# Sparse attention with a dense layer behind it: q and k turned by transposing DMAs instead of by fp32 products

## The chip, the cores and the metric

The kernel runs on one core of a Trainium2 chip. A core has five engines that run side by side, each through its own instructions in order: PE (matrix products, with weight loads shown as PEld), VectorE (DVE in the profile), ScalarE (ACT), GpSimd (POOL) and SyncE (SP), which here only issues DMAs. Data lies in SBUF (128 partitions) and products come out in PSUM banks. The metric is the device time of one execution in microseconds, lower is better. The median of the runs is compared.

## The reference, cut to what matters

Sixty-four heads (batch 8 x 8 heads) of 576 tokens with 64 features go through attention with a threshold: per query only those scores count that lie within tau = 0.02 of the row's largest. The result, in fp32, goes through a dense layer with a leaky ReLU.

```python
scores = scale * np.matmul(q, k.transpose(0, 1, 3, 2))        # 576 x 576 per head
thresh = np.max(scores, axis=-1, keepdims=True) - tau
scores = np.where(scores >= thresh, scores, -1000000000.0)
scores = scores - np.max(scores, axis=-1, keepdims=True)
attn = np.exp(scores)
attn = attn / (np.sum(attn, axis=-1, keepdims=True) + 1e-09)
attn_out = np.matmul(attn, v)
x = attn_out.transpose(0, 2, 1, 3).reshape(B * S, H * D)      # 4608 x 512
h = x @ w_in                                                  # 512 -> 2048
out = np.maximum(0.01 * h, h) @ w_out                         # 2048 -> 512
```

The threshold makes the scores delicate: they have to be near fp32. The kernel gets this from fp16 products by splitting q and k into two fp16 halves, hi and lo (hi = fp16(64 x), lo = fp16(64 x - hi)), and adding hi*hi + lo*hi + hi*lo.

## The kernel before, in words

**Rounds and steps.** Two heads make a pair (32 pairs), since two times 64 features fill 128 partitions. The main loop (L406 on) runs over rounds c of two pairs, and each round over nine steps t. A step takes 128 queries of the two heads of a pair: t = 0 to 3 the first pair's, t = 4 to 7 the second's, t = 8 the last 64 of each. There are 16 rounds with scores and one more that drains what is left. The program is written in the order in which each engine runs it (manual_schedule); no planner moves anything.

**A step.** `s_mm` (L145) multiplies the halves on PE into two PSUM tiles `s`, one per head. There are only two such tiles, so the next step's products wait until this step's have been read. `s_max` (L167) reads one head's tile on VectorE, writes the scaled negative scores `sn` and their row minimum `nmx` (L181), and lets GpSimd add tau: `nth`, one column (L186). ScalarE then takes the exponential, `e` (L191); for some second heads it also does the masking by itself (L197, L201: "direct" in the code). One step later `s_mask` (L206) masks on VectorE (L214: `sn` and `e` from SBUF, `W` out, one instruction for each head that ScalarE hasn't masked, so one or two per step) and SP issues a transposing DMA of `W` into `wT` (L220). In the next round, at t = 3 and 5, `values` (L271) multiplies `wT` by v, and VectorE scales the result into `xT` (L289), of which GpSimd copies 64 columns.

**The dense layer** is cut into units (`h_unit` L296, `out_mm` L310) that fill PE between the score products; `work` (L375) gives each step its number of them by a table of shares.

**q and k.** `load_qk` (L73) loads a pair's q and k in fp32 with tokens on the partitions into one of three `nat` buffers: nine chunks of 128 tokens, four of q, four of k, and one with the last 64 of both. The loads are issued by SP about a round ahead. But the products need features on the partitions. `prep` (L122) turns a pair in two parts, four chunks (i = 0, 512 columns) and five (i = 1, 640 columns): a PE product with the fp32 identity `I32` per chunk (L129) into the PSUM pair "A", then ScalarE writes `hi` from it (L138), and VectorE writes `lo` (L139), put off by the list `soon` to the end of the step. In round c the pairs of the next round are turned at t = 6 (first pair, part 0), 7 (first pair, part 1), 8 (second pair, part 0), and at t = 0 of the following round (second pair, part 1). The PSUM pair "A" also serves `values` and the row sums (`sums_3`, `sums_4`).

The queues in a step: VectorE does `sn`, `sn`, the masks of the step before, then what `soon` holds (`xT`, `lo`). GpSimd does `nth`, `nth`, then small copies and, in even rounds from t = 4 on, the issue of v loads. SP issues the transposes of W, the q and k loads and the output stores, in order.

Of the kernel before, what the change touches and what calls it, by code (L numbers as in the profile page):

```python
# [10 lines left out]
FP16 = mybir.dt.float16  # L11
OP = mybir.AluOpType
AF = mybir.ActivationFunctionType
# [3 lines left out]
def kernel(  # L17
# [10 lines left out]
    nc = tc.nc  # L28
# [3 lines left out]
    NP = B * H // 2  # L32
    NG = H // 2
    NC = NP // 2
    NT = 9
    NJ = d_ff // 128
    QS = 64.0
    BS = 1.0 / (QS * QS * 8.0)
    RS = 1.0 / 2048.0
# [2 lines left out]
    sb = ctx.enter_context(tc.tile_pool(name="sb", bufs=1))  # L42
# [18 lines left out]
    nat, qk, wTs, xTs = {}, {}, {}, {}  # L61
# [49 lines left out]
    soon = []  # L111

    def take(fs):
        r = list(fs)
        fs.clear()
        return r

    def run(fs):
        for f in fs:
            f()  # L120

    def prep(p, i, tag="A", bufs=1):  # L122


        t = nat[p]
        pt = pair_of_banks(tag, bufs).rearrange("p a b -> p (a b)")
        for c in range(4 + i):

            nc.tensor.matmul(  # L129
                out=pt[0:128, ds(c * 128, 128)],  # L130
                lhsT=t[0:128, 4 * i + c, :, :].rearrange("p h d -> p (h d)"),
                rhs=I32[:, :],
                is_transpose=True, skip_group_check=True,
            )
        N = 512 + 128 * i
        hi = sb.tile([128, N], FP16, tag=f"hi{i}", bufs=3, name=f"hi{i}")
        lo = sb.tile([128, N], FP16, tag=f"lo{i}", bufs=3, name=f"lo{i}")
        nc.scalar.activation(out=hi[:, :], in_=pt[:, 0:N], func=AF.Copy, bias=0.0, scale=QS)  # L138
        soon.append(lambda: nc.vector.scalar_tensor_tensor(  # L139
            out=lo[:, :], in0=pt[:, 0:N], scalar=QS, in1=hi[:, :],  # L140
            op0=OP.mult, op1=OP.subtract,
        ))
        qk.setdefault(p, {})[i] = (hi, lo)

    def s_mm(c, t):  # L145


        out = [ps.tile([128, 2, 512], FP32, tag="s", bufs=2, name="s") for _ in range(2)]
        if t < 8:
            srcs = [(2 * c + t // 4, 0, ds(t % 4 * 128, 128), ds(0, 128))]  # L150
        else:
            srcs = [(2 * c + e, 1, ds(576, 64), ds(64 * e, 64)) for e in range(2)]
        for half in range(2):
            for ti, (a, b) in enumerate(((0, 0), (1, 0), (0, 1))):
                for p, i, cols, po in srcs:
                    for h in range(2):
                        r = ds(h * 64, 64)
                        nc.tensor.matmul(  # L158
                            out=out[h][po, half, 0:288], lhsT=qk[p][i][a][r, cols],
                            rhs=qk[p][1][b][r, ds(half * 288, 288)],  # L160
                            start=(ti == 0), stop=(ti == 2), skip_group_check=True,
                        )
        sc[(c, t)] = out
# [146 lines left out]
    def out_mm(key, g_in, part, osb, half, store):  # L310
# [64 lines left out]
    def work(n):  # L375
        for _ in range(min(n, len(units))):
            units.pop(0)[1]()

    with tc.manual_schedule():
        nc.scalar.preload_act_table_set("natural_log_exp_and_others")  # L380
        for i, tail in ((0, 0), (1, 0), (0, 1), (1, 1)):
# [6 lines left out]
            out=sel[:, :, :], in0=I32[:, 0:18].unsqueeze(2).to_broadcast([128, 18, 64]),  # L388
            in1=I32[:, 64:82].unsqueeze(2).to_broadcast([128, 18, 64]), op=OP.add,
# [16 lines left out]
        for c in range(NC + 1):  # L406
            last = c == NC
            for t in range(NT):
                step = c * NT + t
                if c > 1 and c % 2 == 0 and t == 6:  # L410

                    if c % 4 == 2 and c > 2:
                        push_tail(c // 2 - 3, 1)
                    push_main(c // 2 - 1)
                    if c % 4 == 0:
                        push_tail(c // 2 - 2, 0)
                    if last:
                        push_tail(c // 2 - 2, 1)
                if not last:
                    s_mm(c, t)  # L420


                nxt = {6: (2 * c + 2, 0), 7: (2 * c + 2, 1), 8: (2 * c + 3, 0), 0: (2 * c + 1, 1)}
                if c == 0:
                    nxt[0], nxt[1] = (1, 0), (1, 1)
                pi = nxt.get(t)
                if pi is not None and pi[0] >= NP:
                    pi = None
                if c == 0 and t < 2:
                    prep(*pi)  # L430
                    pi = None

                if c > 0 and t in (3, 5):
                    values(c - 1, t // 2 - 1)

                ahead = [share[i % NT] for i in range(step, (c // 2 * 2 + (0 if c % 2 == 0 and t < 6 else 2)) * NT + 6)]
                credit = min(credit, 1.0) + (len(units) - credit) * share[t] / sum(ahead)
                n = min(int(credit + 0.01), len(units))
                credit -= n
                if not last:  # L440


                    direct = tau_f <= 16.0 and (
                        t not in (3, 7) if c < 3 else t in (3, 5) or not any(u[0] for u in units[:n]))
                    s_max(c, t, 0, False)
                if c > 0 and t == 1:
                    sums_1(c - 1)
                work(n - n // 2)
                if pi is not None:
                    prep(*pi)  # L450
                if c > 0 and t in (2, 4):
                    sums_4(c - 1, t // 2 - 1)
                if not last:
# [63 lines left out]
```

## Time and profile before

| what | value |
|---|---|
| median of 3 runs | 540.81 us (540.47 to 541.48) |
| span of the profiled execution | 538.3 us, 12333 instructions |
| PE busy | 497.8 us (92%) |
| VectorE busy | 421.7 us (78%) |
| ScalarE busy | 433.8 us (81%) |
| GpSimd busy | 188.1 us (35%) |
| DMA of SP's queue, share of 16 engines | 72.3% |
| fp32 products that turn q and k (L129) | 288 in all, 9 a pair |
| transposing DMAs (L220) | 144, issue 1.354 us (median), 3.9 us to landing (median) |

The runs time the whole execution; the profile's span is that of one profiled execution, from its first to its last instruction, and lies 2.5 us under the median. An engine's share is an average over the whole span. The granted clock of PE is 0.80 in the first 60 us and 1.00 from about 100 us on, and after about 487 us only the dense layer is left.

In the groups, a row names the line, the engine and the operation, the tile written and the tiles read, shapes and count; then busy time in us and the mean of one in ns; then the idle time of the engine before these instructions and what ended it.

### The profile page before, as it was taken

To read this page: it belongs to the slowest core of one execution; us is meant where nothing else is said; L and a number is where in the kernel's file an instruction comes from. 1 tells how busy PE (TensorE), PEld (TensorE's weight loads), DVE (VectorE), ACT (ScalarE), POOL (GpSimd) and SP (SyncE) were. 2 spreads that over 40 slices of the span, in tenths; PEclk is the share of its full clock that TensorE was granted. 3 is DMA by queue.
4 is the path that set the end of the run, shared out by engine and by line. 5 is a ranking of instruction groups with operands and counts; after the bars stand their busy time and mean duration, and the time that the engine had idled before them with its cause. 6 is when DMAs were issued, how large, how long until landed. Compare 5 with 4: busy or idle time off the path is not lost.

```text
span 538.3 us, 12333 instructions
## 1 busy us (share of the span) xinstructions
PE 497.8 (92%) x4384; PEld 272.8 (51%) x4384; DVE 421.7 (78%) x1106; ACT 433.8 (81%) x765; POOL 188.1 (35%) x430
## 2 busy tenths in 40 slices
PE   5678679899999999999999999999999999999996
PEld 3345454454545565454545566455545566445444
DVE  4897989988899878987899878987899878982000
ACT  3887879899878989889888989889888989884622
POOL 0754556443433334222432234323432234331000
PEclk9676969999999999999999999999999999999999
DMA  6999999998998699778999799777998699654001
GB/s 151 150 202 161 175 182 214 200 180 173 172 165 136 139 169 196 140 137 153 183 155 143 132 182 185 142 135 159 183 155 136 132 187 135 111 89 106 39 40 58
DMA packets 266814, 80.50 MB, mean 150 GB/s; under 512 B 251905, under 2 KB 264193, under 8 KB 266753
## 3 DMA queue, kind: packets, MB, share of 16 engines
q1 hardware_dynamic: 249136, 70.68, 72.3%
q0 software_dynamic: 17536, 8.92, 14.2%
q8 instruction: 34, 0.56, 0.4%
q14 instruction: 28, 0.22, 0.1%
q10 hardware_dynamic: 80, 0.13, 0.1%
HBM read 36.70 MB, written 9.44 MB: 86 GB/s over the span
## 4 chain that ended last, share of the span: by engine, by line
PE 43%; ACT 25%; DVE 16%; issue 8%; DMA 4%; POOL 3%; SPq 0%; DVEq 0%; ACTq 0%; POOLq 0%
PE u L316 13%; DVE sn L181 11%; PE u L301 10%; PE s L158 10%; PE A L279 8%; ACT e L191 7%; ACT far L197 5%; ACT W L201 5%; DVE W L214 3%; ACT gM L305 3%; ACT hi L138 3%; POOL nth L186 3%; DMA nat<-in_q_dram 2%; DVE lo L139 1%; ACT rc L268 1%
## 5 line engine op out<-in xcount | busy, mean ns | idle before, releaser
L181 DVE TENSOR_SCALAR_CACHE_REDUCE sn<-s 128x576 f32<-128x576 f32 x288 | 206.5, 750 | 49.3 <-PE s L158 49.1
L186 POOL TENSOR_SCALAR nth<-nmx 128x1 f32<-128x1 f32 x288 | 127.4, 442 | 251.7 <-DVE sn L181 229.5
L191 ACT ACTIVATE e<-sn,nmx 128x576 f16<-128x576 f32 x196 | 150.5, 769 | 32.4 <-DVE sn L181 32.2
L214 DVE SCALAR_TENSOR_TENSOR W<-sn,nth,e 128x576 f16<-128x576 f32 x196 | 155.6, 814 | 0.0
L301 PE MATMUL u<-xT,win 128*128 128x512 f16 x512 | 128.9, 380 | 2.5 <-ACT gM L305 2.5
L316 PE MATMUL u<-wout,gM 128*128 128x512 f16 x512 | 126.2, 380 | 0.0
L158 PEld LDWEIGHTS <-hi 64*128 64x128 f16 (+1 forms) x1280 | 65.1, 99 | 70.2 <-issue 54.9
L158 PE MATMUL s<-hi,hi 64*128 64x288 f16 x512 | 86.2, 300 | 10.3 <-DVE sn L181 8.8
L158 PE MATMUL s<-lo,hi 64*128 64x288 f16 (+1 forms) x640 | 92.2, 294 | 0.0
L158 PE MATMUL s<-hi,lo 64*128 64x288 f16 (+1 forms) x640 | 92.1, 294 | 0.0
L301 PEld LDWEIGHTS <-win 128*128 128x128 f16 x768 | 58.7, 98 | 56.5 <-issue 20.1
L305 ACT ACTIVATE gM<-u 128x512 f16<-128x512 f32 x128 | 74.6, 588 | 11.7 <-PE u L301 11.7
L197 ACT ACTIVATE far<-sn,nth 128x576 f32<-128x576 f32 x92 | 71.0, 771 | 13.8 <-POOL nth L186 11.6
L201 ACT ACTIVATE W<-far,ntau 128x576 f16<-128x576 f32 x92 | 71.3, 775 | 3.0
L316 PEld LDWEIGHTS <-gM 128*128 128x128 f16 x512 | 44.7, 98 | 51.3 <-issue 12.3
L139 DVE SCALAR_TENSOR_TENSOR lo<-A,hi 128x512 f16<-128x512 f32 (+1 forms) x63 | 47.6, 756 | 14.2 <-ACT hi L138 13.7
L129 PE MATMUL A<-I,nat 128*128 128x128 f32 x283 | 44.6, 288 | 9.9 <-DVE lo L139 4.7
L279 PE MATMUL A<-wT,V 128*64 128x288 f16 x640 | 47.5, 297 | 1.5 <-ACT rc L268 1.1
L129 PEld LDWEIGHTS A<-I,nat 128*128 128x128 f32 x283 | 35.2, 147 | 25.2 <-DVE lo L139 10.0
L138 ACT ACTIVATE hi<-A 128x512 f16<-128x512 f32 (+1 forms) x63 | 40.0, 636 | 7.6 <-PE A L129 7.6
L279 PEld LDWEIGHTS <-V 128*64 128x64 f16 x640 | 36.6, 113 | 11.9 <-issue 8.4
L158 PEld LDWEIGHTS <-lo 64*128 64x128 f16 (+1 forms) x640 | 32.1, 99 | 12.6 <-issue 8.9
(44 smaller groups left out, 292.1 us busy)
## 6 DMA issues: line engine op xcount, KB each, us to landing
nat<-in_q_dram SPq DMA_DIRECT2D x32, 256.0 KB, 3.8
nat<-in_k_dram SPq DMA_DIRECT2D x32, 256.0 KB, 3.9
out_dram<-osb SPq DMA_DIRECT2D x16, 512.0 KB, 3.0
wT<-W SPq DMA_TRANSPOSE x144, 3.9
V<-in_v_dram POOLq DMA_DIRECT2D x8, 256.0 KB, 6.1
win<-in_moe_w_in_dram POOLq DMA_DIRECT2D x16, 128.0 KB, 5.2
V<-in_v_dram POOLq DMA_DIRECT2D x16, 128.0 KB, 4.7
wout<-in_moe_w_out_dram POOLq DMA_DIRECT2D x16, 128.0 KB, 4.3
```

Of the source, the lines that this page charges most:

```text
L129: nc.tensor.matmul(out=pt[0:128, ds(c * 128, 128)], lhsT=t[0:128, 4 * i + c, :, :].rearrange("p h d -> p (h d)"), rhs=I32[:, :], is_transp ...
L158: nc.tensor.matmul(out=out[h][po, half, 0:288], lhsT=qk[p][i][a][r, cols], rhs=qk[p][1][b][r, ds(half * 288, 288)], start=(ti == 0), stop= ...
L181: nc.vector.tensor_scalar(out=sn[:, h, :].rearrange("p (a b) -> p a b", a=2), in0=s_[:, :, 0:288], scalar1=-BS, scalar2=None, op0=OP.mult, ...
L186: nc.gpsimd.tensor_scalar(out=nth[:, h:h + 1], in0=nmx[:, h:h + 1], scalar1=1.0, scalar2=tau_f, op0=OP.mult, op1=OP.add,)
L191: nc.scalar.activation(out=e[:, h, :], in_=sn[:, h, :], func=AF.Exp, bias=nmx[:, h:h + 1], scale=-1.0,)
L197: nc.scalar.activation(out=far[:, :], in_=sn[:, h, :], func=AF.Prelu, bias=nth[:, h:h + 1], scale=-1.0, alpha=BIG,)
L201: nc.scalar.activation(out=w[:, ds(h * 576, 576)], in_=far[:, :], func=AF.Exp, bias=ntau[:, 0:1], scale=1.0, accum_out=dens[c][:, 2 * t + ...
L214: nc.vector.scalar_tensor_tensor(out=w[:, ds(h * 576, 576)], in0=sn[:, h, :], scalar=nth[:, h:h + 1], in1=e[:, h, :], op0=OP.is_le, op1=OP ...
L279: nc.tensor.matmul(out=t[ds(h * 64, 64), half, 0:288], lhsT=vb[:, g, h, kb, :], rhs=wT[:, 4 * h + kb, ds(e * 576 + half * 288, 288)], star ...
L301: nc.tensor.matmul(out=t[:, ts(j, N)], lhsT=w_in16[:, gi, ts(j0 + j, 128)], rhs=xs[gi], start=(gi == 0), stop=(gi == NG - 1), skip_group_c ...
L305: nc.scalar.activation(out=g_out, in_=t[:, 0:nj * N].rearrange("p (j n) -> p j n", j=nj), func=AF.Prelu, bias=0.0, scale=1.0, alpha=0.01)
L316: nc.tensor.matmul(out=t[:, :], lhsT=g_in(j), rhs=w_out16[:, j, :], start=(j == 0), stop=(j == NJ - 1), skip_group_check=True,)
```

## The change

The first four pairs stay as they were (`PEP = 4`). From the fifth on a pair is split where it lies, with tokens on the partitions: `split` writes `hn` = fp16(64 x) on GpSimd from `nat`, and by `soon` VectorE writes `ln` from `nat` and `hn`, in two parts of 512 and 640 columns. `turn` then has SP issue two transposing DMAs, `hn` into `hi` and `ln` into `lo`, each of 128 x 1152. In round c the next round's first pair is split at t = 4 and 5 and turned at the end of t = 5; the second is split at t = 7 and 8 and turned at the end of t = 0 of the next round. `hn` and `ln` have one buffer each. `hi` and `lo` are now one tile per pair of nine chunks, in three buffers, where there were two tiles of four and five chunks; the score products read the same columns. Of the 288 fp32 products 36 are left, of the 64 ScalarE copies 8; VectorE has as many instructions as before, GpSimd has 56 more, SP issues 56 DMAs more.

```diff
+    PEP = 4
...
+    halves = {}
+
+    def turned(p):
+        if p not in qk:
+            qk[p] = [sb.tile([128, 9, 128], FP16, tag=n, bufs=3, name=n) for n in ("hi", "lo")]
+        return qk[p]
...
-        hi = sb.tile([128, N], FP16, tag=f"hi{i}", bufs=3, name=f"hi{i}")
-        lo = sb.tile([128, N], FP16, tag=f"lo{i}", bufs=3, name=f"lo{i}")
-        nc.scalar.activation(out=hi[:, :], in_=pt[:, 0:N], func=AF.Copy, bias=0.0, scale=QS)
+        hi, lo = (x.rearrange("p c q -> p (c q)")[:, ds(512 * i, N)] for x in turned(p))
+        nc.scalar.activation(out=hi, in_=pt[:, 0:N], func=AF.Copy, bias=0.0, scale=QS)
...
+    def split(p, i):
+
+        if i == 0:
+            halves[p] = [sb.tile([128, 1152], FP16, tag=n, bufs=1, name=n) for n in ("hn", "ln")]
+        hn, ln = halves[p]
+        cols = ds(512 * i, 512 + 128 * i)
+        t = nat[p].rearrange("p c h d -> p (c h d)")
+        nc.gpsimd.tensor_scalar(out=hn[:, cols], in0=t[:, cols], scalar1=QS, scalar2=1.0,
+                                op0=OP.mult, op1=OP.mult)
+        soon.append(lambda: nc.vector.scalar_tensor_tensor(
+            out=ln[:, cols], in0=t[:, cols], scalar=QS, in1=hn[:, cols],
+            op0=OP.mult, op1=OP.subtract,
+        ))
+
+    def turn(p):
+
+        for x, n in zip(turned(p), halves.pop(p)):
+            nc.sync.dma_start_transpose(out=x[:, :, :], in_=n[:, :])
...
-                            out=out[h][po, half, 0:288], lhsT=qk[p][i][a][r, cols],
-                            rhs=qk[p][1][b][r, ds(half * 288, 288)],
+                            out=out[h][po, half, 0:288], lhsT=x[a][r, cols],
+                            rhs=x[b][r, ds(512 + half * 288, 288)],
...
-                if pi is not None and pi[0] >= NP:
+                if pi is not None and pi[0] >= PEP:
                     pi = None
+                si = {4: (2 * c + 2, 0), 5: (2 * c + 2, 1), 7: (2 * c + 3, 0), 8: (2 * c + 3, 1)}.get(t)
+                if si is not None and not PEP <= si[0] < NP:
+                    si = None
+                ti = {5: 2 * c + 2, 0: 2 * c + 1}.get(t)
+                if ti is not None and not PEP <= ti < NP:
+                    ti = None
...
+                if si is not None:
+                    split(*si)
                 if prev is not None:
                     s_mask(*prev)
                     prev = None
                 if not last:
                     prev = (c, t)
                 run(take(soon))
+                if ti is not None:
+                    turn(ti)
```

More of the change, by code (lines that the diff above doesn't have):

```diff
@@ L135, in prep @@
         N = 512 + 128 * i
-        hi = sb.tile([128, N], FP16, tag=f"hi{i}", bufs=3, name=f"hi{i}")
-        lo = sb.tile([128, N], FP16, tag=f"lo{i}", bufs=3, name=f"lo{i}")
-        nc.scalar.activation(out=hi[:, :], in_=pt[:, 0:N], func=AF.Copy, bias=0.0, scale=QS)
+        hi, lo = (x.rearrange("p c q -> p (c q)")[:, ds(512 * i, N)] for x in turned(p))
+        nc.scalar.activation(out=hi, in_=pt[:, 0:N], func=AF.Copy, bias=0.0, scale=QS)
         soon.append(lambda: nc.vector.scalar_tensor_tensor(
-            out=lo[:, :], in0=pt[:, 0:N], scalar=QS, in1=hi[:, :],
+            out=lo, in0=pt[:, 0:N], scalar=QS, in1=hi,
             op0=OP.mult, op1=OP.subtract,
         ))
-        qk.setdefault(p, {})[i] = (hi, lo)
+    def split(p, i):
[13 more added lines that the diff above has]
+            nc.sync.dma_start_transpose(out=x[:, :, :], in_=n[:, :])
     def s_mm(c, t):
@@ L149, in s_mm @@
         if t < 8:
-            srcs = [(2 * c + t // 4, 0, ds(t % 4 * 128, 128), ds(0, 128))]
+            srcs = [(2 * c + t // 4, ds(t % 4 * 128, 128), ds(0, 128))]
         else:
-            srcs = [(2 * c + e, 1, ds(576, 64), ds(64 * e, 64)) for e in range(2)]
+            srcs = [(2 * c + e, ds(1088, 64), ds(64 * e, 64)) for e in range(2)]
         for half in range(2):
             for ti, (a, b) in enumerate(((0, 0), (1, 0), (0, 1))):
-                for p, i, cols, po in srcs:
+                for p, cols, po in srcs:
+                    x = [y.rearrange("p c q -> p (c q)") for y in qk[p]]
                     for h in range(2):
```

## The prediction

> **What bounds the kernel now.** I read the busy shares first, then the costliest groups, then the waits, and last one whole round of the attention loop, step by step. The shares: PE works almost all the time, and VectorE and ScalarE are not far behind it.
>
> ```profile
> PE 497.8 (92%) x4384; PEld 272.8 (51%) x4384; DVE 421.7 (78%) x1106; ACT 433.8 (81%) x765; POOL 188.1 (35%) x430
> ```
>
> The groups that the change touches are the fp32 products that turn q and k, their ScalarE and VectorE halves, and GpSimd's one-column `nth`:
>
> ```profile
> L186 POOL TENSOR_SCALAR nth<-nmx 128x1 f32<-128x1 f32 x288 | 127.4, 442 | 251.7 <-DVE sn L181 229.5
> ...
> L139 DVE SCALAR_TENSOR_TENSOR lo<-A,hi 128x512 f16<-128x512 f32 (+1 forms) x63 | 47.6, 756 | 14.2 <-ACT hi L138 13.7
> L129 PE MATMUL A<-I,nat 128*128 128x128 f32 x283 | 44.6, 288 | 9.9 <-DVE lo L139 4.7
> ...
> L138 ACT ACTIVATE hi<-A 128x512 f16<-128x512 f32 (+1 forms) x63 | 40.0, 636 | 7.6 <-PE A L129 7.6
> ```
>
> Now stretches that run from one step's first `sn` to the next step's: t = 4 to 8 of round 6, then t = 0 to 3 of round 7 (start:end, length, then busy time and instructions of PE, weight load, VectorE, ScalarE, GpSimd; clock, DMA share, GB/s).
>
> ```profile
> 196.38:199.37 2.99, 2.96 (x50) 2.55 (x50) 2.18 (x6) 2.96 (x7) 1.59 (x3) 1.00 1.49 243
> 199.37:203.62 4.25, 4.18 (x65) 3.51 (x65) 3.59 (x9) 3.53 (x7) 1.56 (x5) 1.00 0.89 133
> 203.62:206.73 3.11, 3.11 (x25) 1.67 (x25) 2.79 (x7) 2.88 (x7) 1.82 (x4) 1.00 1.37 248
> 206.73:209.98 3.25, 3.25 (x38) 1.90 (x38) 3.01 (x7) 3.18 (x6) 1.52 (x3) 1.00 1.52 132
> 209.98:213.42 3.44, 3.44 (x26) 1.76 (x26) 2.79 (x7) 3.44 (x8) 1.53 (x3) 1.00 0.99 191
> 213.42:216.99 3.57, 3.57 (x28) 1.98 (x27) 3.57 (x11) 3.29 (x7) 1.10 (x3) 1.00 1.02 195
> ...
> sum 31.04, PE 30.36 PEld 18.10 DVE 27.48 ACT 27.45 POOL 12.10; mean PE 3.37 PEld 2.01 DVE 3.05 ACT 3.05 POOL 1.34
> ```
>
> PE fills 30.36 of a round's 31.04 us; but VectorE fills 27.48, so it has 3.6 us a round to lose before it is the bound. And it runs strictly in order. VectorE and GpSimd within t = 7, the fourth stretch:
>
> ```profile
> 207.42 0.75 DVE L181 TENSOR_SCALAR_CACHE_REDUCE sn<-s 128x576 f32<-128x576 f32 x1
> 208.09 0.08 DVE L181 DVE_READ_ACCUMULATOR sn<-s 128x1 f32 x1
> 208.09 0.81 DVE L214 SCALAR_TENSOR_TENSOR W<-sn,nth,e 128x576 f16<-128x576 f32 x1
> 208.84 0.08 DVE L214 DVE_READ_ACCUMULATOR W<-sn,nth,e 128x1 f32 x1
> 208.99 0.82 DVE L139 SCALAR_TENSOR_TENSOR lo<-A,hi 128x640 f16<-128x640 f32 x1
> ...
> 207.66 0.19 POOL L186 TENSOR_SCALAR nth<-nmx 128x1 f32<-128x1 f32 x1 [1.11 <-ACT W L201]
> 208.26 0.70 POOL L186 TENSOR_SCALAR nth<-nmx 128x1 f32<-128x1 f32 x1 [0.41 <-DVE sn L181]
> ```
>
> See the two `nth`: one column each, 0.19 us while VectorE does `sn`, 0.70 us while it does a mask (L214), ending at 208.96 with it. GpSimd gets nothing done beside a mask.
>
> **The change part by part.** It concerns 28 of 32 pairs: 56 splits and 56 turns, in rounds 1 to 14.
>
> *Removed from PE:* in the third stretch two runs of four L316 products start at 203.52 and, past four L129 products, at 204.83: 1.31 us, of which four products alone take 0.88 (203.52 to 204.40). So four turns cost 0.43 us, five by the same reading in t = 7 0.54. A round loses 2 x (0.43 + 0.54) = 1.94 us of PE, 14 rounds 27 us: the most that can be won.
>
> *Removed from ScalarE:* 56 `hi` copies of 0.636 us, 36 us. ScalarE's idle time is ended by `sn` and PE, so I count this at nothing; PE and VectorE cover it.
>
> *Moved on VectorE:* the halving stays, as `ln` instead of `lo`. Start to start `lo` takes 0.61 us (512 columns) and 0.74 (640); reading SBUF on both sides, like L214 (576 columns, 0.74 start to start), `ln` should cost the same. But it moves from t = 6, 7, 8, 0 to t = 4, 5, 7, 8, and now it waits for GpSimd.
>
> *Added on GpSimd:* a split of 512 or 640 columns, queued behind the step's second `nth`, hence free 2.28 us after the step's first `sn` (208.96 + 0.05 against 206.73), when the mask is over. Its price has no row. From below: 128x128 affine select 0.291 us against 0.185 for a one-column `nth` gives 0.83 ns a column (the 128x64 copy, 0.236, gives 0.8): 0.61 and 0.72 us. From above: the same operation on 18 columns (0.218) gives 1.94 ns a column: 1.18 and 1.43. I take the low ones, because 128 columns are nearest in size.
>
> The page GPSIMD Engine Reference of the Trainium skill (section Performance versus the Vector engine) says 512 elements take 769 ns in a well unrolled loop, between my ends; by it the splits would cost some 0.77 and 0.96 us and the sum below would be about 11 us higher; no row here shows a split.
>
> *The new wait:* `ln` waits for the split of its own step. Behind it on VectorE stands the next step's `sn`, for which PE's next scores wait. GpSimd's result reaches VectorE 0.07 us after its end (L235 to L240). Step lengths set by VectorE, first `sn` to next:
> - t = 4 and 7: 2.28 + 0.61 + 0.07 + 0.61 = 3.57 us; with two masks 0.74 more, 4.31.
> - t = 8: 2.28 + 0.72 + 0.07 + 0.74 = 3.81; two masks 4.55.
> - t = 5: one mask 3.81 again; two masks 4.55. The `xT` product (0.67) runs meanwhile.
> - t = 6 and 0: no halving left. One mask leaves 2.1, so the loop `sn`, `sn` (1.36), scores on PE (0.9) and their hand-overs sets some 2.4; two masks 2.84.
>
> Against the stretches: 3.57 + 4.55 + 2.4 + 3.57 + 3.81 + 2.84 = 20.74 where 20.61 stood. (These steps have 1, 2, 1, 1, 1 and 2 masks.) The same six of the next rounds: 21.04 against 20.03 (masks 1, 2, 1, 2, 1, 1), 21.48 against 20.69 (1, 1, 1, 2, 2, 2), 20.30 against 19.70 (1, 2, 1, 1, 1, 1). Mean +0.63 us; rounds repeat in this pattern, so 14 x 0.63 = +9 us. The steps t = 1 to 3 hold neither turns nor splits and keep their length. PE's gain of t = 6 and 0 is spent in t = 4, 7 and 8.
>
> *Added on SP:* 56 transposes. Issue 1.354 us each (median of `wT`), 5.4 us a round; SP now waits over 15 us a round for masks and scores, so this fits. SP is in order: turns stand right behind a step's `wT` transposes and ahead of q/k loads, which run a round ahead. Data: three transposes in the drain took some 1.8 us each at a DMA share of 0.8 to 1.0; four more add up to 7 us a round to queues already 87% shared.
>
> *The single `hn`/`ln` buffer:* the split of t = 7 may overwrite `hn` only when the turn of t = 5 has landed. From t = 5's first `sn`: mask over at 2.84, `wT` issued until 4.2, turn of `hn` lands 3.9 later (median) at 8.1, of `ln` 1.35 behind at 9.45. Wanted: 4.55 + 2.4 + 2.28 = 9.23 and, for `ln`, 9.9. It fits by 0.5 to 1 us, but landings range from 3.2 to 9.0 and there are more of them. Between 0 and 1.5 us a round I take 0.5: +7 us. Other buffers (three of `hi`/`lo`, six of W) leave four or more steps.
>
> Sum: span 538.3 + 9 + 7 = 554.3; the median of the runs, 540.81, lies 2.5 above the profiled span, so 556.8: 557 us.
>
> **The rivals.**
> 1. *VectorE's idle time takes the waits.* If the three unhidden waits (0.87 + 0.87 + 0.98 us = 2.7) fall into the 3.6 us that VectorE now idles, a round needs VectorE 30.1 and PE 28.4 of 31.04: 0.9 less, 14 rounds 13 us, 528 us. For it: 49 us of idle before `sn` until PE's scores. Against: that idle lies mostly in t = 1, 4 and 5; only two score tiles stand between the engines. It decides where the four splits of a round give back the 0.63 us above, that is where the wait for one is under some 0.71 us instead of 0.87.
> 2. *The split is slow* (1.18/1.43): 0.57 + 0.71 + 0.57 + 0.71 more a round, 36 us: 593. For it: the same operation's own slope; against: 17 columns make it.
> 3. *Turns land late.* With 1.5 to 2 us a round more at t = 7, 557 + 21 = 578. For it: stretches with DMA shares of 1.4 to 1.5; against: shares fall to 0.5 in others.
> 4. *The turns' cost is hidden and PE's gain lost elsewhere*: about 541.
>
> **How the numbers follow.** Forecast (546 to 568) 0.43, slow split 0.18, late turns 0.14, gain by rival 1 0.20, no change 0.05. A difference under 0.2% (1.1 us) can't be told from none. Slower: 0.43 + 0.18 + 0.14 = 0.75; faster 0.20; same 0.05. The range reaches from rival 1's 528 to rival 2's 593, with about 0.1 left out on each side.
>
> **What would show it.** Right: `ln` idle before, ended by `hn` on GpSimd, 0.3 to 1 us in each of t = 4, 7, 8, some 30 us in all; PE under 90% busy; PE waiting for `sn`; splits of 0.6 to 0.75 us. Waits of `hn` for a DMA would be the buffer. Wrong: splits that end while masks run, a VectorE without idle time ahead of `ln`, or rounds under 30 us.

## The result, and the profile after

The changed kernel takes 589.44 us (median of 4 runs, 588.58 to 591.52), the kernel before 540.64 us in the same comparison (539.92 to 541.48): a ratio of 1.0911, 95% interval 1.0887 to 1.0935. Ratios, here and below, leave out any run that took over 1.5% longer than the fastest of its kernel, so a ratio can lie a little under what the medians give. The forecast had the sign and not the size: +16 us were forecast, +49 us came. The range of 528 to 593 us holds the time, but its upper end was there for another reason, a slow split, which did not come.

The head of the page of after, its busy shares and the granted clock of PE in 40 slices:

```profile
span 588.1 us, 11908 instructions
...
PE 497.7 (85%) x4132; PEld 255.6 (43%) x4132; DVE 422.8 (72%) x1106; ACT 406.9 (69%) x709; POOL 237.9 (40%) x486
...
PEclk9568579799989999799989999798989999899999
```

PE has lost its 252 products and its instructions are still busy for as long as before (497.8 us then): the clock now falls again and again in the main loop, where it stood at 1.00 before, so that the same products last longer. No engine is busy over 90% of the span any more. The span of 588.1 us is 49.8 longer than before's 538.3, and PE's share of it fell from 92 to 85%.

What the engines wait for instead, from the groups of the page and from the list of waits (time in all, times, longest, in us):

```profile
L160 DVE SCALAR_TENSOR_TENSOR ln<-nat,hn 128x512 f16<-128x512 f32 (+1 forms) x56 | 42.5, 759 | 71.0 <-POOL hn L158 44.3
...
L158 POOL TENSOR_SCALAR hn<-nat 128x512 f16<-128x512 f32 (+1 forms) x56 | 46.0, 822 | 40.0 <-DMA hi<-hn 24.0
```

```profile
PE s L184 <- DVE sn L207: 65.2, 65, 5.5
DVE ln L160 <- POOL hn L158: 44.3, 41, 5.7
...
DVE ln L160 <- DMA lo<-ln: 26.7, 6, 7.1
...
POOL hn L158 <- DMA hi<-hn: 24.0, 6, 5.8
...
PEld L184 <- DMA hi<-hn: 17.7, 8, 3.6
```

Read these against each other. VectorE stands 71.0 us before `ln`, where some 30 were forecast. But 26.7 of them are six waits of up to 7.1 us for the turn of `lo`, and GpSimd's 24.0 are six waits for the turn of `hi`: the buffers `hn` and `ln` were still being read. By the trace GpSimd's six lie in t = 7 of rounds 1, 2, 6, 10, 12 and 14, VectorE's in t = 7 of rounds 2, 6, 7, 10, 11 and 12. In rounds 4 and 8 the split of t = 7 begins 0.13 us after the turn has landed as well, though the trace names no releaser there. So it is mostly the even rounds. Two odd-round stretches first (t = 6 and 7 of round 5), then t = 5, 6, 7, 8 of round 6 and t = 0 of round 7; columns as in the stretches of before (length; PE, weight load, VectorE, ScalarE, GpSimd; clock, DMA share, GB/s):

```profile
196.91:199.23 2.32, 1.92 (x17) 0.91 (x15) 2.18 (x7) 0.84 (x2) 1.07 (x3) 1.00 1.09 206
199.23:202.80 3.57, 3.57 (x38) 1.72 (x38) 2.80 (x8) 3.51 (x7) 1.50 (x3) 1.00 0.94 182
...
222.31:226.58 4.27, 4.27 (x64) 3.25 (x60) 4.27 (x12) 3.66 (x8) 2.80 (x5) 1.00 1.31 197
226.58:228.90 2.32, 2.27 (x19) 1.01 (x17) 2.18 (x8) 1.17 (x3) 1.71 (x5) 1.00 1.30 243
228.90:235.99 7.09, 4.75 (x41) 2.09 (x41) 2.79 (x8) 4.35 (x8) 2.69 (x5) 0.97 1.23 183
235.99:239.78 3.79, 2.69 (x14) 1.19 (x14) 2.91 (x8) 2.41 (x4) 2.19 (x4) 0.50 0.93 131
239.78:243.43 3.65, 3.65 (x20) 1.37 (x19) 2.92 (x9) 2.52 (x4) 1.10 (x3) 0.64 1.27 259
```

t = 7 took 3.57 us in round 5, to the hundredth what was forecast, and 7.09 in round 6, with no more work on VectorE (2.80 and 2.79 us). Behind the long step the granted clock is 0.50. The timeline of SP, GpSimd and VectorE tells what happened in between (start, duration; in brackets the idle time before):

```profile
197.00 1.31 SPq L168 DMA_TRANSPOSE hi<-hn  x1
198.40 1.39 SPq L168 DMA_TRANSPOSE lo<-ln  x1
...
201.54 0.62 POOL L158 TENSOR_SCALAR hn<-nat 128x512 f16<-128x512 f32 x1
```

```profile
226.03 2.98 SPq L246 DMA_TRANSPOSE wT<-W  x1
229.11 1.33 SPq L168 DMA_TRANSPOSE hi<-hn  x1
230.53 2.68 SPq L168 DMA_TRANSPOSE lo<-ln  x1
...
230.42 0.70 POOL L212 TENSOR_SCALAR nth<-nmx 128x1 f32<-128x1 f32 x1 [0.41 <-DVE sn L207]
234.48 0.62 POOL L158 TENSOR_SCALAR hn<-nat 128x512 f16<-128x512 f32 x1 [3.36 <-DMA hi<-hn]
...
230.25 0.81 DVE L240 SCALAR_TENSOR_TENSOR W<-sn,nth,e 128x576 f16<-128x576 f32 x1
...
235.38 0.69 DVE L160 SCALAR_TENSOR_TENSOR ln<-nat,hn 128x512 f16<-128x512 f32 x1 [4.30 <-DMA lo<-ln]
235.99 0.75 DVE L207 TENSOR_SCALAR_CACHE_REDUCE sn<-s 128x576 f32<-128x576 f32 x1
```

In round 5 SP issues the turn of `hn` 4.35 us after t = 5's first `sn` (192.65), and GpSimd's split follows its second `nth` without a wait. In round 6 the same turn goes out 6.80 us after it (222.31), since SP had been issuing one transfer after the other, and the transposes of W ahead of it took up to 2.98 us to issue instead of 1.3; GpSimd then stands 3.36 us until it has landed, VectorE 4.30 us, and the next `sn` behind both.

Where the 49.8 us lie can be summed by step. The length of a step is taken from its first `sn` to the next step's on VectorE's timeline; the table has the sum over rounds 1 to 14, less the same sum of before, in us. It covers the experiments of the next section too.

| kernel | t=0 | 1 | 2 | 3 | 4 | 5 | 6 | 7 | 8 | sum |
|---|---|---|---|---|---|---|---|---|---|---|
| after | -8.3 | 0.0 | 0.3 | -0.3 | 11.7 | 1.5 | -10.0 | **44.4** | 10.4 | 49.7 |
| two buffers | -2.6 | 0.8 | 0.7 | 0.8 | 11.7 | 1.5 | -9.4 | 5.0 | **32.4** | 40.9 |
| `ln` a step later | -1.5 | 0.8 | 0.7 | 4.9 | 2.8 | 1.4 | -6.7 | -2.1 | **25.3** | 25.5 |
| before + transposes | 0.1 | 0.0 | 0.0 | **16.6** | 1.6 | -0.7 | 0.0 | 0.0 | 0.0 | 17.7 |
| no turning | -8.8 | 0.1 | 0.0 | -0.7 | -0.1 | 0.0 | -7.0 | -8.0 | -3.6 | -28.2 |
| half the turns | 2.0 | -0.1 | 0.0 | 1.5 | 2.7 | 1.4 | -7.0 | -8.0 | **17.5** | 10.1 |
| half, early | -0.1 | **26.9** | 3.3 | -0.5 | -0.1 | 0.0 | -7.0 | -8.0 | 2.9 | 17.3 |
| half, between | -0.1 | -0.2 | 3.1 | 0.9 | 2.9 | -1.6 | -6.9 | -8.0 | 2.9 | -7.0 |

### The profile page after: what moved, and what is told of

It is laid out like the page before. It is cut to its first block, busy times and chain, and to the rows that moved or that the text cites. A ratio compares the mean times of both kernels' runs of the same rounds, so it can differ in the third digit from the quotient of the medians.

```text
span 588.1 us, 11908 instructions
## 1 busy us (share of the span) xinstructions
PE 497.7 (85%) x4132; PEld 255.6 (43%) x4132; DVE 422.8 (72%) x1106; ACT 406.9 (69%) x709; POOL 237.9 (40%) x486
## 3 DMA queue, kind: packets, MB, share of 16 engines
q1 hardware_dynamic: 315440, 87.20, 82.8%
## 5 line engine op out<-in xcount | busy, mean ns | idle before, releaser
L184 PE MATMUL s<-hi 64*128 64x288 f16 (+1 forms) x640 | 112.2, 310 | 66.9 <-DVE sn L207 65.2
L327 PE MATMUL u<-xT,win 128*128 128x512 f16 x512 | 135.1, 402 | 4.6 <-ACT osb L353 2.2
L184 PEld LDWEIGHTS <-hi 64*128 64x128 f16 (+1 forms) x1280 | 75.7, 103 | 122.8 <-issue 91.6
L184 PE MATMUL s<-lo,hi 64*128 64x288 f16 (+1 forms) x640 | 103.9, 308 | 0.0
L184 PE MATMUL s<-hi,lo 64*128 64x288 f16 (+1 forms) x640 | 103.7, 308 | 0.0
L160 DVE SCALAR_TENSOR_TENSOR ln<-nat,hn 128x512 f16<-128x512 f32 (+1 forms) x56 | 42.5, 759 | 71.0 <-POOL hn L158 44.3
L223 ACT ACTIVATE far<-sn,nth 128x576 f32<-128x576 f32 x92 | 71.0, 772 | 28.2 <-POOL nth L212 26.2
L158 POOL TENSOR_SCALAR hn<-nat 128x512 f16<-128x512 f32 (+1 forms) x56 | 46.0, 822 | 40.0 <-DMA hi<-hn 24.0
L184 PEld LDWEIGHTS <-lo 64*128 64x128 f16 (+1 forms) x640 | 36.0, 102 | 26.8 <-issue 22.9
L353 ACT ACTIVATE osb<-u 128x512 f32<-128x512 f32 x35 | 20.4, 584 | 22.5 <-PE u L342 22.5
L315 DVE TENSOR_TENSOR xT<-A,rc 128x576 f16<-128x576 f32 x32 | 24.1, 753 | 8.8 <-PE A L305 8.6
```

Source lines behind the costliest of these rows:

```text
L158: nc.gpsimd.tensor_scalar(out=hn[:, cols], in0=t[:, cols], scalar1=QS, scalar2=1.0, op0=OP.mult, op1=OP.mult)
L184: nc.tensor.matmul(out=out[h][po, half, 0:288], lhsT=x[a][r, cols], rhs=x[b][r, ds(512 + half * 288, 288)], start=(ti == 0), stop=(ti == 2 ...
L223: nc.scalar.activation(out=far[:, :], in_=sn[:, h, :], func=AF.Prelu, bias=nth[:, h:h + 1], scale=-1.0, alpha=BIG,)
L327: nc.tensor.matmul(out=t[:, ts(j, N)], lhsT=w_in16[:, gi, ts(j0 + j, 128)], rhs=xs[gi], start=(gi == 0), stop=(gi == NG - 1), skip_group_c ...
```

## The experiments

**Two buffers for the halves.** If the single `hn`/`ln` buffer is the cost, a second one gives it back. Room for it was made by one `sn` buffer less.

```diff
-            halves[p] = [sb.tile([128, 1152], FP16, tag=n, bufs=1, name=n) for n in ("hn", "ln")]
+            halves[p] = [sb.tile([128, 1152], FP16, tag=n, bufs=2, name=n) for n in ("hn", "ln")]
...
-            sn = sb.tile([128, 2, 576], FP32, tag="sn", bufs=3, name="sn")
+            sn = sb.tile([128, 2, 576], FP32, tag="sn", bufs=2, name="sn")
```

> hn and ln get two buffers each; sn gives up one of its three to make room. In the profile after, the step t = 7 takes 6.45 us on average where GpSimd's and VectorE's own work gives 3.57 (one mask) or 4.31 (two), about 38 us over the 14 rounds. Theory (the single buffer): t = 7 falls to 3.57/4.31 in every round, the waits of hn and ln for a DMA go away, the time falls by some 38 us to 551, 10 us above the kernel before. Rival (the DMA queues are simply too full): the turns are as late as ever, PE waits for hi instead at t = 4 and t = 0, and the time stays above 575.

577.51 us, ratio to before 1.0701 (1.0654 to 1.0747): 12 us came back of the 38 expected. t = 7 went to 3.56 us with one mask and 4.03 with two in every round from the fourth on, as the theory of the buffer says. But t = 8 took 5.2 to 8.1 us in five of the six even rounds from the fourth on, against 3.79 in the odd ones. The waits of this kernel name who stands there now:

```profile
PEld L184 <- DMA hi<-hn: 25.8, 8, 8.4
PE s L184 <- DMA hi<-hn: 21.7, 5, 7.9
...
PEld L184 <- DMA lo<-ln: 12.0, 9, 2.6
```

These are the score products of the next round's first step, which PE does in t = 8 and which read the turned pair. So the buffer only chose who waits; the turn of t = 5 is late itself, and what made it late was not touched.

**Who makes the turn late: v loads or stores.** Even rounds differ from odd ones by the v loads that GpSimd issues, and by output stores. Two experiments moved one each.

```diff
-                if c % 2 == 0 and c > 0 and t >= 4 and c // 2 < B:
-                    load_v(c // 2, t - 4)
+                if c % 2 == 1 and t >= 4 and c // 2 + 1 < B:
+                    load_v(c // 2 + 1, t - 4)
```

> The v loads of a batch are issued one round earlier, in odd rounds instead of even ones; all else as in the changed kernel (one buffer). In the profile after, t = 7 is late in even rounds (6.4 to 9.9 us) and hardly in odd ones (3.6 to 5.5). Theory (v loads delay the W transposes and turns that SP issues beside them): the lateness moves to the odd rounds, even rounds come down to 3.6 to 4.5 us, the total stays within 10 us of 589. Rival (output stores or the order on SP make it): even rounds stay above 6 us at t = 7 and the odd ones stay below 5.5.

588.98 us, ratio 1.0921 (1.0870 to 1.0971): the same time as after. But the lateness moved: from 34.66 us a round in even rounds and 31.83 in odd ones (rounds 4 to 14) to 32.86 and 33.87. t = 7 grew to 5.9 to 7.3 us in the odd rounds and stayed over 4.7 in all, so the even rounds did not come down to the 3.6 to 4.5 us expected. The v loads are a part of what makes the turns late, not the whole, and wherever they lie something is late.

```diff
-                nc.sync.dma_start(
+                nc.scalar.dma_start(
...
-                eng = nc.scalar if e == 1 and b0 == B - 2 else nc.sync
+                eng = nc.scalar
```

> All output stores are issued from ScalarE's queue instead of SP's, so that no W transpose or turn stands behind a store that waits for ScalarE's copy; one buffer. Theory (stores ahead of the turn on SP): t = 7 of rounds 4, 8 and 12, where a store stands before the turn, falls by 2 to 4 us each, total 577 to 583. Rival (full data queues): t = 7 in these rounds is unchanged and the total is 589 within 4 us.

With the output stores issued by ScalarE: 589.73 us, 1.0940 (1.0899 to 1.0981). t = 7 of rounds 4, 8 and 12 still takes 7.66, 8.13 and 8.86 us (9.22, 8.49 and 8.95 in after). That the stores stand ahead of the turns in SP's order is not the main cause: t = 7 falls by 6 us over the 14 rounds, and the other steps give 5 of it back.

**`ln` one step later, splits earlier.** This goes after the other loss, the steps that VectorE sets while it waits for the split of the same step, and gives the second pair's turn more time. It keeps the two buffers.

```diff
-        soon.append(lambda: nc.vector.scalar_tensor_tensor(
+        later.append(lambda: nc.vector.scalar_tensor_tensor(
...
-                si = {4: (2 * c + 2, 0), 5: (2 * c + 2, 1), 7: (2 * c + 3, 0), 8: (2 * c + 3, 1)}.get(t)
+                si = {3: (2 * c + 2, 0), 4: (2 * c + 2, 1), 6: (2 * c + 3, 0), 7: (2 * c + 3, 1)}.get(t)
...
-                ti = {5: 2 * c + 2, 0: 2 * c + 1}.get(t)
+                ti = {5: 2 * c + 2, 8: 2 * c + 3}.get(t)
...
                 run(take(soon))
+                soon.extend(take(later))
```

> Two buffers as in e1; the splits are made a step earlier (t = 3, 4, 6, 7) and ln stays a step behind its split (t = 4, 5, 7, 8), so VectorE finds hn ready; the second pair is turned at t = 8 instead of t = 0. Theory (the loss is the single buffer and the wait of ln for the split of its own step; nothing else is dear): steps t = 4 and 7 to 0 become 2.6 to 3.5 us, the 27 us of PE work that went away show, 515 to 525 us. Rival (VectorE or the DMA queues bound it all the same): 535 us or more.

566.16 us, 1.0481 (1.0461 to 1.0502), not the 515 to 525 of the theory. The unhidden waits for the split are gone: t = 4 falls from +11.7 to +2.8 us over the rounds. What is left is in the main the wait of PE for turned halves in t = 8 of the even rounds (5.7 to 8.2 us in rounds 4 to 12):

```profile
PEld L184 <- DMA hi<-hn: 19.6, 8, 5.2
...
PEld L184 <- DMA lo<-ln: 13.5, 8, 3.2
...
PE s L184 <- DMA hi<-hn: 13.1, 5, 4.7
```

Two smaller losses are of other kinds. In t = 3 of rounds 6, 10 and 14 (4.35 to 4.67 us) PE waits 1.0 to 1.3 us for `wT`. In t = 0 of rounds 5, 9 and 13, behind a long t = 8, PE waits for nothing; it is busy all the time at a granted clock of 0.55 to 0.60 (round 5; before took 3.57 us there, at 1.00):

```profile
168.27:173.06 4.79, 4.79 (x21) 1.72 (x21) 2.92 (x8) 2.63 (x4) 1.10 (x3) 0.55 1.03 197
```

**Issue or data?** From here the q and k loads of the fifth pair on were given to ScalarE's queue, so that SP has less to issue:

```diff
-            nc.sync.dma_start(
+            (nc.scalar if p > 3 else nc.sync).dma_start(
```

> e4 (566 us) with the q and k loads from the fifth pair on issued by ScalarE's queue instead of SP's, so that SP issues only transposes and stores: some 5 us a round less of SP's time, the same bytes. Theory A (SP's in-order issue bounds it): turns land in time, PE stops waiting for hi and lo, 515 to 535 us. Theory B (the data engines bound it, whoever issues): 555 us or more, PE's waits for hi and lo remain some 50 us.

566.92 us, 1.0456 (1.0406 to 1.0506), against 566.16 without it, though what SP's issues take fell from 444 to 369 us. Its one trace, of its longest run (572.68 us), shows why that is not enough. In rounds 6 and 10 the turn of `hn` now goes out 4.3 us after t = 5's first `sn`, instead of 8.3 and 6.9, but still takes 6.6 and 6.8 us to land; in rounds 4, 8 and 12 it still goes out at 7.1, 6.5 and 7.1 (8.3, 8.1 and 7.2 with the loads on SP). So SP's time to issue the loads is not what is short. The Trainium skill, *DMA: Bandwidth & Descriptors*, section "Issuing engines are not separate DMA queues", says that DMAs of all issuing engines run on the same 16 engines and interleave there; this run agrees with it.

**The transposes alone.** The kernel before, with 56 transposes more that nobody reads: `W` of four steps a round is transposed once more into a tile of its own. PE turns q and k as before.

```diff
         nc.sync.dma_start_transpose(out=wTs[c][:, :, ds(q0, 128)], in_=w[:, :])
+        if 1 <= c <= 14 and t in (0, 4, 5, 8):
+            x = sb.tile([128, 9, 128], FP16, tag="extra", bufs=2, name="extra")
+            nc.sync.dma_start_transpose(out=x[:, :, :], in_=w[:, :])
```

> The kernel before, with q and k still turned on PE; in rounds 1 to 14 four of a round's nine W transposes are issued twice, the second time into a tile that nobody reads. So it has the changed kernel's 200 transposes and nothing else of the change. Theory (13 transposes a round beside the loads are more than SP's queue and the data engines get through in 30 us): W buffers come free late, values wait for wT, and the time is 555 to 575 us. Rival (the transposes are hidden where nobody waits soon for them; only the turn's short deadline is dear): 540 to 545 us.

558.33 us, 1.0324 (1.0288 to 1.0359): 18 us for transfers without a reader. The table puts 16.6 of them into t = 3, where the first product with v reads `wT`, and 15.1 of these lie in three of the 14 rounds (3, 7 and 13). The list of waits has there, with no counterpart of that size before:

```profile
PE A L282 <- DMA wT<-W: 12.2, 6, 4.6
PEld L282 <- DMA wT<-W: 12.0, 5, 4.9
```

So four more transposes a round cost time in themselves, without any split, buffer or turn. Here the trace shows SP's order at work. The last transpose of W that these products need went out 12.2, 9.2 and 9.8 us after the first `sn` of rounds 3, 7 and 13, instead of 3.7, 2.9 and 2.9 in before, and then landed in 3.4 to 4.7 us, where before's three took 3.2 to 4.9. What came late was the issue, with the extra transposes ahead of it in SP's queue.

**What there is to gain.** The kernel before, with the turning of the pairs from the fifth on left out:

```diff
+        if p >= 4:
+            qk[p] = qk[1 + p % 3]
+            return
```

> The kernel before with the turning of q and k left out from the fifth pair on (products, hi and lo alike; the scores of these pairs are taken from the halves of pairs 1 to 3), and no DMA in its place. Theory (PE's products are worth their 27 us, VectorE's and ScalarE's share adds a little): 505 to 518 us, the floor for any way to take the turning off these engines. Rival (another engine holds the round at 30 us): 530 us or more.

513.96 us, 0.9506 (0.9475 to 0.9536). This is 26.6 us less than before, with the `hi` and `lo` copies left out as well; I had put "the most that can be won" at 27, for PE alone. PE is still 92% busy, at 28.3 us a round.

**Cheaper loads.** With the rearranged q and k loads of 1 KB pieces, the same bytes go in fewer packets (290107 in all against 333115), at the cost of two `ln` instructions for each part. The rest is as in the kernel with `ln` a step later.

```diff
+                r = r.rearrange("p (h c d) -> p h c d", h=2, d=64)[:, :, 0:4, :]
+                nc.sync.dma_start(out=r, in_=h2[:, 0:512, :].rearrange("h (p c) d -> p h c d", c=4))
```

> As e4 (566 us), but from the fifth pair on q and k are loaded head by head into nat, so that a piece read from memory is 1 KB instead of 256 B; the split restores the order (two instructions for each ln, one per head: some 0.1 us each more on VectorE). Same bytes, a quarter of the packets. Theory (the time that loads and transposes take together on the data engines is what makes the turns late): fewer packet-microseconds, PE's waits for hi and lo fall from some 57 us to under 25, 535 to 552 us. Rival (the transposes alone are slow, or their issue): 560 us or more.

562.54 us, 1.0419 (1.0375 to 1.0462): some 4 us, and the two intervals just touch. The four rows of PE and its weight loads that wait for turned halves still sum to 56 us (57 before that; the trace is of the longest of its runs, 567.39 us). Fewer packets of loads do not bring the turns in time.

**Half the turns.** The even pairs go by DMA, the odd ones by PE as before: eleven transposes a round instead of thirteen. One buffer is then enough; `ln` stays one step behind its split, by `later` as above.

```diff
-                if pi is not None and pi[0] >= PEP:
+                if pi is not None and (pi[0] >= NP or pi[0] >= PEP and pi[0] % 2 == 0):
...
-                si = {4: (2 * c + 2, 0), 5: (2 * c + 2, 1), 7: (2 * c + 3, 0), 8: (2 * c + 3, 1)}.get(t)
+                si = {3: (2 * c + 2, 0), 4: (2 * c + 2, 1)}.get(t)
...
-                ti = {5: 2 * c + 2, 0: 2 * c + 1}.get(t)
+                ti = {5: 2 * c + 2}.get(t)
```

> e4 with only every second pair (4, 6, 8, ...) split and turned by DMA; pairs 5, 7, ... are turned on PE as in the kernel before. hn and ln have one buffer again, sn three. 11 transposes a round instead of 13. Theory (the DMA path is overfull with 13 a round and just keeps up with 11): the waits of PE for hi and lo go, half of PE's gain (13 us) stays: 525 to 534 us, faster than both kernels. Rival (any turn by DMA is late): 541 us or more.

551.82 us, 1.0207 (1.0172 to 1.0242), not the 525 to 534 expected. In t = 6 and 7 PE's gain stays: they are 15 us shorter over the rounds. But t = 8 takes 17.5 us more, nearly all in even rounds (4.0 to 9.4 us there), waiting for the turn issued three steps before.

**Half, and early.** The same, with both splits at t = 0 and the turn at t = 1, seven steps ahead of its use:

```diff
-                si = {3: (2 * c + 2, 0), 4: (2 * c + 2, 1)}.get(t)
+                si = {0: [(2 * c + 2, 0), (2 * c + 2, 1)]}.get(t, [])
...
-                ti = {5: 2 * c + 2}.get(t)
+                ti = {1: 2 * c + 2}.get(t)
```

> As e7 (every second pair by DMA, 11 transposes a round), but the pair is split at t = 0, its ln written at t = 1 and its turn issued at the end of t = 1, seven steps ahead of the first product that needs it instead of four. In e7 (552 us) the scores of t = 0 waited for the turn, mostly in even rounds. Theory (11 transposes a round fit on average; the short deadline costs the rest): those waits go, half of PE's gain stays: 525 to 533 us, faster than both kernels. Rival (11 transposes and the loads are over what the data queues carry in a round): the turn is late all the same, 541 us or more.

558.37 us, 1.0336 (1.0312 to 1.0360), slower, but for a reason of my own making. No wait for `hi` or `lo` is left. In odd rounds from the fifth on t = 1 takes 6.3 to 7.9 us instead of 4.0. GpSimd's timeline of this kernel in round 7:

```profile
225.22 1.09 POOL L158 TENSOR_SCALAR hn<-nat 128x512 f16<-128x512 f32 x1
228.78 0.72 POOL L158 TENSOR_SCALAR hn<-nat 128x640 f16<-128x640 f32 x1 [2.47 <-DMA nat<-in_k_dram]
229.58 0.22 POOL L254 TENSOR_SCALAR d<-den 128x18 f32<-128x18 f32 x1
```

The split stands in order ahead of `d`, the first step of the row sums, and waits for a load that has not landed (SP issued it at 225.31); VectorE's reciprocal waits 2.59 us for `d`, with the second `sn` of the step behind it. Nothing that GpSimd computes is long here; the queue is held by a wait.

The same with all turns early and the 1 KB loads:

```diff
-                ti = {5: 2 * c + 2, 8: 2 * c + 3}.get(t)
+                ti = {1: 2 * c + 2, 7: 2 * c + 3}.get(t)
...
+                si = {0: [(2 * c + 2, 0), (2 * c + 2, 1)], 5: [(2 * c + 3, 0)], 6: [(2 * c + 3, 1)]}.get(t, [])
```

> As e10, with both pairs of a round by DMA and earlier: the first split at t = 0 and turned at t = 1, the second split at t = 5 and 6 and turned at t = 7, so that seven and six steps lie between a turn and its first use. Theory (with the loads made cheaper, 13 transposes a round fit, and with long deadlines no engine waits for a turn): near the floor of 514, 517 to 530 us. Rival (13 transposes a round are too many whatever the deadlines): rounds of 31 us, 545 us or more.

573.96 us, 1.0629 (1.0593 to 1.0666): of the waits for `hi` and `lo` only two are left, 0.9 us in all, and t = 1 takes 4.8 to 8.9 us by the same order of GpSimd's queue (41 us over the rounds).

**Half, between.** From the last two: a turn needs more than three steps, and the splits have to stand behind the row sums, in steps where VectorE has room for `ln`.

```diff
-                si = {0: [(2 * c + 2, 0), (2 * c + 2, 1)]}.get(t, [])
+                si = {1: [(2 * c + 2, 0)], 3: [(2 * c + 2, 1)]}.get(t, [])
...
-                ti = {1: 2 * c + 2}.get(t)
+                ti = {4: 2 * c + 2}.get(t)
```

> Eleven transposes a round as in e7 and e9 (the even pairs from the fifth on by DMA, the odd ones by fp32 products), but each piece where the step lengths of e9 leave room: GpSimd's split of part 0 at t = 1 (behind the row sums, not ahead of them), its ln at t = 2; the split of part 1 at t = 3, its ln at t = 4; the turn at the end of t = 4, four steps before the scores that want it. Theory (the turns cost time only where something is soon waiting for them, and e9 lost its time to the order of GpSimd's queue alone): t = 1 of the odd rounds falls from 6.3-7.9 us back to 4.0, t = 2 grows from 2.93 to some 3.15 and t = 4 from 2.6-3.0 to some 2.95, no wait for hi or lo; rounds of 29.3 to 30 us, where before has 29.8 to 30.8: 530 us, faster than before. Rival (the queues are late whatever the order: eleven transposes a round are too many beside the v loads): t = 8 or t = 0 wait for hi and lo in even rounds, as in e7, 541 us or more.

534.73 us (532.52 to 537.47), 0.9904 (0.9875 to 0.9932): 1% faster than before, and faster than after. t = 1 is back at 3.67 and 4.0 us, and GpSimd's queue in round 7 now runs without a wait for a load:

```profile
217.46 0.19 POOL L212 TENSOR_SCALAR nth<-nmx 128x1 f32<-128x1 f32 x1 [1.26 <-DVE sn L207]
217.73 0.22 POOL L261 TENSOR_SCALAR r<-rr 128x18 f16<-128x18 f32 x1
218.18 0.79 POOL L212 TENSOR_SCALAR nth<-nmx 128x1 f32<-128x1 f32 x1 [0.23 <-DVE r L266]
219.05 1.09 POOL L158 TENSOR_SCALAR hn<-nat 128x512 f16<-128x512 f32 x1
```

The turns themselves are no faster. For the tile `hn`, what its turn took to issue and to land (min/median/max) in this kernel:

```profile
L168 SPq DMA_TRANSPOSE hi<-hn x14: 1296/1806/4082, 53.6 to 438.4; - x14
...
DMA to landing us min/median/max: 3.3/5.3/7.7
```

and in after:

```profile
L168 SPq DMA_TRANSPOSE hi<-hn x28: 1247/1355/3166, 58.4 to 511.3; - x28
...
DMA to landing us min/median/max: 3.3/3.7/7.1
```

The median landing is 5.3 us here and 3.7 in after: the faster kernel has the later turns. It just asks for them four steps after the issue, and no wait for `hi` or `lo` is in its list. The head of its page:

```profile
PE 489.2 (92%) x4258; PEld 262.2 (49%) x4258; DVE 421.2 (79%) x1106; ACT 419.1 (79%) x737; POOL 213.0 (40%) x458
...
PEclk9987659999999999999999999999999999999999
```

PE is the bound again, at a granted clock of 1.00 from 100 to 480 us. Of half of the 26.6 us that leaving the turning out brings, 13.3, some 5.6 are kept. By the table t = 6 and 7 gain 14.9; `ln` at t = 2 and t = 4 gives back 3.1 and 2.9 (0.29 us of it more than expected in each odd t = 2, which holds two masks: 3.44 us instead of 3.15), and t = 8 another 2.9, which I did not look into. My expectation of 530 us was 5 low; round 3 alone took 31.24 us, over a us above what I allowed any round.

## Why the prediction was wrong in size, step by step

- **PE's 27 us.** Right in size: 26.6 without any turning, though that run leaves out VectorE's and ScalarE's part as well. And right that they are not to be had when VectorE sets the steps.
- **ScalarE's 36 us at nothing.** No run took the `hi` copies away alone. ScalarE's share fell from 81 to 69% and nothing that it did bounded a long step.
- **The split on GpSimd, 0.61 and 0.72 us.** Right where it runs beside no second mask: the shortest of each form are 0.617 and 0.723 us. Beside one it takes up to 1.2, as `nth` takes 0.70 instead of 0.19; by form the means are 0.684 and 0.959. The rival of a slow split (1.18 and 1.43 us throughout) falls. The Trainium skill (*GPSIMD Engine Reference*, "Performance versus the Vector engine") gives 769 ns for 512 elements; the unhindered 512 columns here take 617, so the measurement decides for the lower figure.
- **The step lengths set by VectorE.** Right: t = 4 came out at 3.56 against 3.57, t = 5 and 8 at 3.80 against 3.81 with one mask and 4.26 to 4.27 against 4.55 with two, t = 6 and 0 at 2.3 to 2.9 against 2.4 to 2.84, but for four t = 0 (the clock, below). In the table this is everything but the waits of t = 7: 49.7 less the 38 below leaves 12, where 9 was forecast.
- **VectorE's idle time takes the waits (rival 1).** It fell. It needed a wait under 0.71 us for each split; t = 4 alone lost 11.7 us over 14 rounds, 0.84 a round.
- **"The single hn/ln buffer ... Between 0 and 1.5 us a round I take 0.5: +7 us."** This is the step that failed. t = 7 lost 41.6 us over 3.57 us a round in the 14 rounds; 3.7 of that is the second mask in five of them, so 38 us, 2.7 a round, nearly twice the upper end. The time line behind it (turn issued at 4.2 us, landed at 8.1, wanted at 9.23) holds in rounds 5, 9 and 13, where the turn was issued at 4.35 to 4.37 us and t = 7 took 3.56 or 3.57. In the even rounds from the second on it went out at 6.0 to 9.1 and took 5.2 to 7.1 us to land, on the mean of these seven 3.0 us later and 2.1 us longer than I had priced.
- **"SP now waits over 15 us a round for masks and scores, so this fits."** The reason behind it. Idle time summed over a round was taken for room at a certain point of it. The issue time of 1.354 us and the landing of 3.9 were medians of nine transposes a round; I noted the range of landings, 3.2 to 9.0, and that more transposes would come, and priced both, with the buffer, at those 0.5 us. With thirteen a round the queue's share of the 16 engines went from 72.3 to 82.8%. The extra transposes alone cost 18 us; a second buffer, another engine for the loads, another one for the stores and cheaper loads brought 12, 0, 0 and 4. What is left as the cause is the transposes themselves: late issue in SP's order, as in the run with the extra ones, and long landings, as in the run with the loads from ScalarE. Whether one sets off the other is not shown; no run issued the turns from another queue than SP's.
- **The rival of late turns** had the mechanism, at 1.5 to 2 us a round and a chance of 0.14. It was the forecast's own step with the bound drawn too close.
- **The clock.** Not foreseen: behind long waits PE's granted clock falls to 0.50 and 0.64 in the stretches above. In t = 8 of round 6 this costs nothing (3.79 us, as forecast), but in t = 0 of round 7 PE is busy all of 3.65 us at 0.64, where 2.84 were forecast; t = 0 of rounds 5 and 9 took 3.16 and 3.68 us, busy throughout at 0.67 and 0.56, and that of round 3 took 3.23 at 0.64, where 2.4 were forecast. So some 3 us of the 49, by this sum, can be put down to the clock; no run separates it.

What stays open: why a transpose's issue stretches from 1.3 to 3 us and its landing from 3.3 to 7 in some places (the last section shows what goes with the long landings). Which of the neighbours (q and k loads, v loads, stores) does it in which proportion was not separated beyond the v loads' part.

## What to carry to other kernels

A transfer's median landing is a fact about the load at that time; when a change adds transfers, price each by who waits for it soonest, and give it a deadline at the far end of the landings seen, not at the median. A buffer given to a late transfer moved most of the wait to its reader; what took it away here was fewer transfers and more steps between the issue and the reader. SP's queue is in order too: transfers that nobody waited for delayed those behind them. When work moves to an in-order engine, look at what it itself may wait for there, and put it behind whatever others wait for: with half of the splits t = 1 and 2 lost 30 us when these stood ahead of the row sums, and t = 2 and 4 some 6 when they stood behind them.

## What the runs showed of the hardware that was not expected

**Groups of packets that take over a us.** In the kernel with `ln` a step later, 160 to 165 us, in 40 slices of 0.125 us each, the busy tenths of the DMA engines and what they moved, then a queue of the same view, and two stretches of it (columns as above):

```profile
DMA  8000006999999999990000000005999999999999
GB/s 16 6 8 8 8 6 154 270 195 193 201 195 197 290 274 268 274 113 0 0 0 6 8 8 10 10 8 102 281 295 289 295 225 197 199 193 197 193 283 283
...
q8 instruction: 1, 0.02, 1.2%
```

```profile
162.13:162.25 0.12, 0.00 (x0) 0.00 (x0) 0.12 (x3) 0.12 (x1) 0.12 (x1) 1.00 14.49 107
162.25:163.38 1.13, 0.00 (x0) 0.00 (x0) 1.13 (x3) 0.98 (x2) 0.64 (x1) 1.00 0.05 6
```

From 162.25 to 163.38 hardly a packet starts, though the turns of `hn` (issued at 157.68) and `ln` (160.19, its issue lasting 3.40 us) are under way, between stretches of 190 to 295 GB/s. The engines are not idle in it: these views book a packet's whole time where it starts, hence the share of 14.49. The packet records of the trace show 21 packets of 256 B that start at 162.14 to 162.20, take 1.3 us each, where the median from 159 to 165 us is 0.018, and end together at 163.44 to 163.49.

Such groups (at least twelve packets of 256 B, each over 0.5 us) do not come from the change: 32 of them lie between 60 and 520 us in before and 34 in after. But they go with late landings. Of the 14 first pairs' turns in after, the eight with a group in flight took 5.2 to 7.1 us to land, and the six others 3.3 to 3.4 but for one (5.3, in round 1). The groups in turn go with another queue: 22 of the 34 begin within 1.3 us behind the start of a 16 KB packet of the queue that the page calls `instruction`, of which there are 27 in that time; by chance it would be some three (18 of 32 groups in before, with 32 such packets). No run varies these packets, so what causes the groups is not shown.

**A transpose is many packets.** The 56 more of them put 66304 packets more on SP's queue (249136 before, 315440 after), 1184 each for 0.295 MB, so some 250 bytes a packet. And transposes that no one reads cost 18 us in a kernel whose queue had a share of 72%: a mean share well under 100% was no sign here that the next transfer is free.
